# A gated recurrence with a highway layer behind it: a second new order of all operations

## The chip, the cores and the metric

The kernel runs on one core of one Trainium2 chip. The core has TensorE (PE in the profile; PEld is its weight load), VectorE (DVE), ScalarE (ACT), GpSimd (POOL) and SyncE (SP), which here issues nearly all transfers. Each engine works through a queue of its own, in the order in which the program put the instructions there, and waits at semaphores for the others. The metric is the time of one execution on the device in microseconds, the median of several runs; less is better.

## The reference

```python
def _attn_ref(x, f_logit, lower_bound):          # x, f_logit: (4, 6336, 256)
    sig = 1.0 / (1.0 + np.exp(-f_logit))
    f = lower_bound + (1.0 - lower_bound) * sig
    i = 1.0 - f
    h = np.zeros((B, D))
    for t in range(S):
        h = f[:, t] * h + i[:, t] * x[:, t]
        y[:, t] = h

def _moe_ref(x, w_h, w_t, b_t):                  # x = y as (25344, 256)
    H = np.maximum(x @ w_h, 0.0)
    T = 1.0 / (1.0 + np.exp(-(x @ w_t + b_t)))
    return T * H + (1.0 - T) * x
```

Four sequences of 6336 tokens go through a linear recurrence over time, one for each of 256 channels. Its result goes through a highway layer with two 256 x 256 matrices. Reading x and f_logit and writing the output moves 78 MB.

## The kernel before

The 25,344 tokens are cut into 29 **units**: two of 2 blocks of 128 tokens, three of 4 blocks, twenty-two of 8 blocks (units 5 to 26), one of 4 and one of 2. A full unit has 1024 tokens. The 256 channels are two halves of 128, so most operations exist twice per unit. An operation is written as a letter, the unit and the half: `f20.1` is operation f of unit 20 for half 1.

- `l`, `x` (line 257, or 253 for units 0 and 1, which share one transfer): SP loads f_logit and x, tokens on the partitions. `wh` and `wt` load the matrices.
- `u` (line 269): ACT makes sigmoid(-f_logit), which is 1 - sig.
- `b` (line 277): u times x, on POOL, or on DVE where the order has a `v` behind the name.
- `i` (line 285) and `p` (line 305): PE transposes u and b, so that channels lie on the partitions and time runs along the columns. Both write into two PSUM banks, a0 and a1.
- `f` (line 296 on ACT, 294 on DVE with `v`): the forget gate from the transposed u. It needs `ncc` (line 196), which is made from the transposed lower bound (`pc`, `cc`).
- `s` (line 324): DVE runs the scan over time; unit n needs unit n-1. The profile names it TENSOR_TENSOR_SCAN, the lists of the order below SCALAR_TENSOR_TENSOR y.
- `z` and `g` (line 336, and 111 for the second 512 columns): PE multiplies with w_t and w_h. `WHa` and `WTa` (line 224) scale the matrices on ACT first; `IW` (line 208) subtracts the identity from w_h on POOL.
- `t` (line 349): ACT's sigmoid of z. `d` (line 353): DVE's maximum with g.
- `e` (line 359): d times t, on POOL, or on DVE with `v`, in one to three column pieces per unit.
- `o` (lines 381, 382): PE transposes y (times `diag`, which holds cc) and d back and adds them. `c` (line 394 on ACT, 392 on DVE with `v`): the copy out of PSUM. `w` (line 398): SP stores four blocks, half a megabyte (128 KB in unit 28).
- `k*m`: m dummy matmuls on zeros in front of the next PSUM tile (lines 122 and 111).

What sets the order is one string, `order` (lines 49 to 95), a list of 848 such names. The loop at line 401 walks through it and calls `do_<letter>` for each; `pin` keeps every engine's queue in this order. The number behind a colon is the slot: the buffer or PSUM bank that the result goes into, so an operation also waits until the earlier owner of its slot has been read. [...]

Of the kernel before, what the change touches and what calls it, by code (L numbers as in the profile page):

```python
# [53 lines left out]
e1.0v x6:5 b3.0:7 z2.0:1 b4.0:1 f3.0:3 p3.1:1 t2.0:2 d2.0:2 g2.1:0 i4.1:0 o0.0:2 z2.1:1 f4.1:0 s3.1:6 b4.1:0 d2.1 c0.0:0 t2.1 p3.0:1
i4.0:0 f4.0:2 s3.0:7 l7:0 e2.0v p4.0:0 o1.0:2 e2.1 u5:1 p4.1:1 s4.0:0 z3.0:0 l8:1 g3.0:1 t3.0:1 b5.1:3 c1.0:1 i5.1:0 g3.1:0 s4.1:1
i5.0:1 f5.1:1 g4.0:2 d3.0:0 b5.0:2 e3.0 d3.1 p5.1:0 d4.0:1 z4.1:1 z4.0:0 f5.0:3 o2.0:2 p5.0:1 u6:2 c2.0:2 x7:0 s5.1:2 i6.1:0 t4.1:0
g4.1:2 z3.1:1 s5.0:3 f6.1:2 t3.1 t4.0 x8:1 l9:2 d4.1 b6.1:4 p6.1:0 s6.1:4 u7:3 z5.1:1 i6.0:1 f6.0:0 t5.1:2 b6.0:5 g5.0:2 i7.1:0 z5.0:0
p6.0:1 d5.0:2 g5.1:2 u8:0 e4.1 e3.1 e4.0 f7.1v:1 t5.0 l11:3 s6.0:5 d5.1 i7.0:0 o4.0:1 l10:4 x9:2 f7.0:3 b7.0:6 x10:3 p7.0:1 c4.0:3
z6.1:0 b7.1:7 i8.1:0 g6.0:2 b8.1:1 t6.1:1 s7.0:0 b8.0:0 g6.1:1 k*0:a1 d6.0:1 f8.1:2 p7.1:1 e5.2 s7.1:1 d6.1 z6.0:0 i8.0:0 o3.0:2 u9:1
e5.1v t6.0 g7.1:0 i9.0:1 e6.2v e5.0v f8.0:0 e6.1v z7.0:1 c3.0:4 z7.1:2 i9.1:0 w0.0 f9.0:3 w1.0 e6.0v b9.1:3 p8.1:1 t7.0:0 o5.0:1 t7.1  # L60
o5.1:2 f9.1:1 u10:2 c5.0:0 p8.0:0 x11:4 b9.0:2 w4.0 w2.0 d7.1:0 e7.1 g7.0:0 s8.1:6 i10.0:1 o6.0:1 s8.0:7 l13:5 p9.1:0 c5.1:1 z8.0:2
d7.0 f10.0v:2 l12:0 w5.1 u11:3 t8.0:2 e7.2 z8.1:0 w3.0 x12:5 s9.1:2 c6.0:3 b10.0:4 i11.0:1 f11.0:0 w5.0 l14:1 t8.1 g8.1:2 e7.0 p9.0:0
d8.1:2 o6.1:1 l15:2 u13:0 k*1:a1 s9.0:3 g8.0:2 i10.1:1 b11.0:5 d8.0 c6.1:2 f10.1:1 o7.1:0 w6.0 p10.0:0 e8.1 g9.1:1 b10.1:6 c7.1:1
z9.1:2 u12:1 t9.1:1 s10.0:4 i13.1:1 d9.1:1 f13.1:3 g9.0:0 x13:0 p10.1:0 s10.1:5 o7.0:1 e8.0 e8.2 c7.0:4 o8.1:2 p11.0:1 d9.0 i11.1:0
l16:4 z10.1:1 b12.1:7 g10.1:0 c8.1:0 s11.0:0 f11.1:2 z9.0:2 d10.1:0 b11.1:1 p11.1:0 i12.0:1 o8.0:0 u14:2 b12.0:0 t9.0 f12.0:1 w8.1 w6.1
w7.0 s11.1:1 t10.1:0 g10.0:2 k*0:a1 i12.1:1 e9.0 z10.0:1 p12.0:0 b13.0:3 d10.0 f12.1v:0 c8.0:3 u15:3 z11.1:0 z11.0:2 p12.1:1 t10.0
o9.1:1 t11.0:2 b13.1:2 s12.0:6 s12.1:7 t11.1 x14:1 i13.0:0 g11.0:2 d11.0:2 f13.0:2 w8.0 o9.0:0 p13.0:0 c9.1:0 i14.0:1 c9.0:2 s13.0:2
z12.1:1 g11.1:2 e10.0 f14.0:1 d11.1 t12.1:1 b14.0:4 x15:2 u16:1 i14.1:1 b15.1:6 g12.1:0 o10.1:1 z12.0:2 f14.1:0 d12.1:1 p13.1:0 b14.1:5
c10.1:4 g12.0:0 e11.0v i16.0:1 w7.1 l18:3 t12.0 x16:3 s13.1:3 f16.0:2 o10.0:1 c10.0:3 o11.1:2 c11.1:1 p14.0:0 i15.0:1 b15.0:1 w9.1
l17:5 l20:0 d12.0 z13.0:1 g13.1:0 f15.0:3 t13.0:0 p14.1:1 s14.0:4 o11.0:2 i15.1:0 d13.1:0 z13.1:1 s14.1:5 g13.0:0 u18:0 d13.0 f15.1:1  # L70
i18.0:0 b16.0:0 w10.1 p15.1:1 w11.1 x17:4 c11.0:0 t13.1 f18.0:0 z14.0:2 e12.0 t14.0:2 z14.1:0 s15.1:0 p15.0:0 w10.0 t14.1 s15.0:1
o12.0:1 p16.0:1 g14.0:2 c12.0:4 g14.1:0 d14.0:2 i16.1:0 u17:2 w11.0 d14.1 b16.1:7 e13.0 o12.1:1 b17.0:3 s16.0:6 b17.1:2 e14.0 z15.1:2
f16.1:1 c12.1:1 i17.0:0 t15.1:1 f17.0:3 g15.1:0 o13.0:1 d15.1:1 x18:5 p16.1:1 z15.0:2 i17.1:0 g15.0:0 c13.0:3 s16.1:7 l19:1 u20:3
o13.1:1 x19:0 f17.1:2 c13.1:0 p17.0:1 t15.0 b18.0:4 i18.1:0 f18.1:1 g16.0:1 d15.0 g16.1:0 s17.0:2 w12.1 w12.0 d16.0:0 p17.1:1 z16.1:2
z16.0:1 d16.1 u19:1 t16.1:0 x20:1 i19.0:0 t16.0 o14.0:0 f19.0:3 b18.1:5 o14.1:2 l21:2 c14.0:1 s17.1:3 c14.1:4 w9.0 i19.1:1 p18.1:0
z17.1:1 e15.0v z17.0:0 e16.0v g17.1:2 w13.1 b19.0:6 x21:2 f19.1:2 p18.0:1 t17.0:2 t17.1 b19.1:1 s18.1:4 o16.1:0 i20.0:0 u21:2 l22:4
b20.0:0 d17.1:2 s18.0:5 f20.0:1 g17.0:1 o16.0:2 w14.1 w13.0 c16.0:2 i21.1:1 p19.0:0 z18.0:2 d17.0 f21.1:0 c16.1:0 b20.1:7 t18.0:1
p19.1:1 z18.1:1 l23:3 b21.0:3 g18.1:0 t18.1 s19.0:6 s19.1:7 p20.0:0 o15.0:2 b21.1:2 e17.0 o15.1:1 u22:0 d18.1:0 i21.0:1 s20.0:0 g18.0:0
c15.0:4 c15.1:3 z19.0:2 w16.1 d18.0 g19.0:1 x22:3 i20.1:0 f21.0:3 d19.0:1 w15.1 t19.0:0 p20.1:1 w16.0 f20.1:2 z19.1:0 o17.1:2 e18.0
t19.1 g19.1:1 p21.0:0 o17.0:0 s20.1:1 d19.1 w14.0 i22.1:1 b22.1:5 s21.0:2 u23:1 c17.1:0 g20.1:1 o18.0:2 f22.1:1 e19.0 i22.0:1 l24:5  # L80
c17.0:3 x23:4 d20.1:2 w17.1 p21.1:0 o18.1:0 w15.0 c18.0:2 f22.0:2 s21.1:3 g20.0:2 i23.0:1 c18.1:1 u24:2 z20.0:1 t20.0:2 f23.0:3 p22.1:0
d20.0 z20.1:0 b22.0:4 l25:0 w17.0 x24:5 o19.1:2 c19.1:0 s22.1:4 g21.0:1 i23.1:1 p22.0:0 z21.0:2 b23.1:6 w18.1 t20.1 d21.0:0 f23.1:0
b23.0:1 g21.1:1 e20.0 o19.0:0 s22.0:5 t21.0:1 b24.0:0 l26:1 l28:2 c19.0:4 d21.1 i24.0:1 f24.0:1 p23.1:0 z22.1:2 g22.0:1 t22.1:0 z21.1:0
s23.1:6 d22.0:1 i24.1:1 b24.1:7 u25:3 p23.0:0 o20.1:2 s23.0:7 t21.1 x25:0 g22.1:1 c20.1:3 o20.0:0 d22.1 p24.0:0 z22.0:2 e21.0 f24.1:2
c20.0:1 w19.1 b25.0:3 e22.1 g23.1:1 z23.1:0 w20.0 s24.0:0 t22.0 b25.1:2 d23.1:2 p24.1:1 l27:4 s24.1:1 u26:0 t23.1:2 w20.1 i25.0:0
g23.0:2 f25.0:0 o21.1:1 o21.0:0 e22.2 c21.1:0 c21.0:1 i25.1:0 x26:1 p25.0:1 d23.0 f25.1:3 u28:1 g24.1:1 z24.0:2 t24.0:1 s25.0:2 i26.0:0
b26.0:5 d24.1:0 z24.1:0 p25.1:1 f26.0:1 t24.1 e22.0v z23.0:2 x28:2 t23.0 i28.0:0 f28.0:2 o22.0:1 g24.0:0 o22.1:2 c22.0:3 s25.1:3 d24.0
i28.1:0 e23.1 e23.0v w19.0 x27:3 u27:2 i26.1:1 e24.0v w21.1 w21.0 f28.1:0 c22.1:4 g25.0:1 e23.2v b26.1:4 e24.2 o23.0:0 w22.0 f26.1:3
p26.0:0 z25.0:2 d25.0:1 c23.0:0 t25.0:0 o23.1:1 w23.0 w22.1 p26.1:1 s26.0:4 z25.1:0 c23.1:1 w18.0 i27.0:0 o24.1:2 g25.1:1 t25.1 e24.1
s26.1:5 f27.0:1 c24.1:3 i27.1:0 f27.1:3 b27.1:6 d25.1 g26.1:0 z26.1:2 z26.0:1 b27.0:1 p27.0:1 w23.1 e25.1 d26.1:2 o24.0:0 e25.0v  # L90
t26.1:2 t26.0 p27.1:0 c24.0:0 b28.0:0 o25.1:2 e25.2 c25.1:4 s27.0:6 e26.2 w24.1 g26.0:1 s27.1:7 o25.0:0 d26.0 c25.0 z27.0:a1 t27.0:1
p28.0:0 o25.3:2 b28.1:7 s28.0:0 e26.0v g27.1:0 z27.1:1 c25.3:2 e26.1 t27.1 p28.1:1 d27.1:0 s28.1:1 w24.0 o25.2:a0 c25.2 o26.3:2 o26.2:1
c26.3:1 g27.0:0 e27.1v d27.0 e27.0v w25.0 o26.1:a0 w25.1 z28.0:a1 o26.0:2 c26.2 c26.1:3 g28.0:1 t28.0:0 g28.1:0 z28.1:a0 o27.1:a1 c26.0
# [345 lines left out]
```

## Time and profile before

| | |
|---|---|
| median of 3 runs | 206.5 us (206.05 to 206.52) |
| profiled execution: its own time | 206.63 us |
| profiled execution: span | 204.8 us |
| PE busy | 190.2 us (93%) |
| DVE busy | 192.0 us (94%) |
| ACT busy | 194.5 us (95%) |
| POOL busy | 171.8 us (84%) |
| moved by DMA | 78.68 MB, mean 384 GB/s |

The span is what the trace covers; the profiled execution's own time is 1.8 us more. In the chain of work that ended last, PE has 39%, DVE 20%, ACT 15%, POOL 13%, and 10% is issue time. "Busy" counts an instruction from its start to its end; neighbours on one engine overlap by a tenth of a microsecond or so, and the start-to-start time is what the queue really spends on one.

### The profile page before, as it was taken

What the parts mean: (1) busy time and instruction counts of PE and PEld (TensorE: products, weight loads), DVE (VectorE), ACT (ScalarE), POOL (GpSimd) and SP (SyncE); (2) the same over time, 40 slices, a digit from 0 to 9 for tenths busy, and PEclk for the clock granted to TensorE, in tenths of its full rate; (3) what the DMA queues carried; (4) which work ended last, traced back from release to release, by engine and by line L of the source; (5) the groups of instructions that cost most, each with busy time, mean ns of one, the idle gap of its engine ahead of it and who ended that gap; (6) DMA issues with size and microseconds to landing.
All of it is one profiled execution on the core that took longest, in us unless ns stands there. A gap on an engine that the chain in (4) does not pass through costs nothing.

```text
span 204.8 us, 4621 instructions
## 1 busy us (share of the span) xinstructions
PE 190.2 (93%) x1818; PEld 131.8 (64%) x1818; DVE 192.0 (94%) x160; ACT 194.5 (95%) x204; POOL 171.8 (84%) x97
## 2 busy tenths in 40 slices
...
GB/s 196 397 422 416 413 426 413 421 413 414 426 426 413 426 415 422 420 426 417 426 413 426 428 410 419 403 346 337 334 403 412 424 324 381 390 187 402 212 307 261
DMA packets 16381, 78.68 MB, mean 384 GB/s; under 512 B 1764, under 2 KB 2536, under 8 KB 10728
## 3 DMA queue, kind: packets, MB, share of 16 engines
...
q10 hardware_dynamic: 8, 0.00, 0.0%
HBM read 52.43 MB, written 25.95 MB: 383 GB/s over the span
## 4 chain that ended last, share of the span: by engine, by line
PE 39%; DVE 20%; ACT 15%; POOL 13%; issue 10%; ACTq 0%; POOLq 0%; DVEq 0%
DVE y L324 11%; POOL bv L277 8%; DVE d L353 6%; PE op L381 6%; PE op L382 6%; ACT o L394 5%; POOL d L359 5%; PE g L336 5%; PE bT L305 5%; ACT f L296 5%; PE z L336 4%; PE g L111 4%; ACT t L349 4%; PE z L111 4%; PE uT L285 4%
## 5 line engine op out<-in xcount | busy, mean ns | idle before, releaser
L277 POOL TENSOR_TENSOR bv<-u,x 128x1024 bf16<-128x1024 f16 (+2 forms) x53 | 104.8, 2007 | 16.3 <-DVE d L359 5.5
L324 DVE TENSOR_TENSOR_SCAN y<-f,y,bT 128x1024 bf16<-128x1024 f16 (+5 forms) x56 | 107.3, 1930 | 0.7 <-PE bT L305 0.2
L359 POOL TENSOR_TENSOR d<-d,t 128x512 bf16<-128x512 bf16 (+2 forms) x31 | 67.2, 2180 | 3.2 <-DVE d L359 2.4
L353 DVE SCALAR_TENSOR_TENSOR d<-y,ncc,g 128x1024 bf16<-128x1024 bf16 (+2 forms) x58 | 63.5, 1108 | 1.0 <-PE g L111 0.4
L349 ACT ACTIVATE t<-z,bt 128x1024 bf16<-128x1024 f32 (+2 forms) x58 | 60.4, 1088 | 1.0 <-PE z L111 0.8
L296 ACT ACTIVATE f<-uT,ncc 128x1024 f16<-128x1024 f16 (+2 forms) x54 | 59.1, 1097 | 1.2 <-PE uT L285 0.9
L394 ACT COPY o<-op 128x1024 f32<-128x1024 f32 (+2 forms) x57 | 54.0, 994 | 0.8 <-PE op L382 0.6
L269 ACT ACTIVATE u<-l 128x2048 f16<-128x2048 f32 (+2 forms) x29 | 50.5, 1745 | 1.7 <-DMA l<-in_f_logit_dram 1.7
L381 PE MATMUL op<-diag,y 128*128 128x128 f16 x396 | 49.3, 219 | 1.1 <-DVE d L353 0.5
L382 PE MATMUL op<-ident_b,d 128*128 128x128 bf16 x396 | 49.4, 219 | 0.0
L382 PEld LDWEIGHTS <-d 128*128 128x128 bf16 x396 | 44.1, 113 | 3.8 <-issue 1.7
L381 PEld LDWEIGHTS <-y 128*128 128x128 bf16 x396 | 44.2, 113 | 2.2
L336 PE MATMUL g<-y,w_sb 128*128 128x512 bf16 (+1 forms) x116 | 40.2, 368 | 0.8 <-ACT o L394 0.3
L336 PE MATMUL z<-y,w_sb 128*128 128x512 bf16 (+1 forms) x116 | 39.9, 368 | 0.3 <-ACT o L394 0.2
L305 PE MATMUL bT<-ident_f,bv 128*128 128x128 f32 x198 | 32.0, 277 | 4.3 <-ACT f L296 1.4
L285 PEld LDWEIGHTS <-u 128*128 128x128 f16 x396 | 26.3, 98 | 13.2 <-issue 4.9
L285 PE MATMUL uT<-ident_h,u 128*128 128x128 f16 x396 | 31.5, 219 | 2.4 <-DVE y L324 0.9
L111 PE MATMUL g<-y,w_sb 128*128 128x512 bf16 x88 | 33.3, 379 | 0.0
L111 PE MATMUL z<-y,w_sb 128*128 128x512 bf16 x88 | 33.3, 379 | 0.0
L336 PEld LDWEIGHTS <-w_sb 128*128 128x128 f16 x232 | 22.3, 98 | 15.2 <-ACT f L296 0.2
L305 PEld LDWEIGHTS bT<-ident_f,bv 128*128 128x128 f32 x198 | 22.1, 141 | 13.1 <-issue 4.4
L111 PEld LDWEIGHTS <-w_sb 128*128 128x128 f16 x176 | 17.2, 98 | 15.9 <-issue 1.8
...
## 6 DMA issues: line engine op xcount, KB each, us to landing
...
l<-in_f_logit_dram SPq DMA_DIRECT2D x22, 1024.0 KB, 14.1
x<-in_x_dram SPq DMA_DIRECT2D x22, 1024.0 KB, 12.1
...
```

Of the source, the lines that this page charges most:

```text
L111: return pe.add_instruction(mybir.InstMatmult(name=nc.get_next_instruction_name(), start_tensor_calc=start, stop_tensor_calc=stop, tile_si ...
L277: shared(pin(e.tensor_mul(bv[:, :nb // 2].rearrange("p k d j -> p k j d"), st[n]["u"][:, :nb, own].rearrange("p (k j) d -> p k j d", j=2), ...
L285: pin(nc.tensor.transpose(uT[:, j * P:(j + 1) * P], st[n]["u"][:, j, h * P:(h + 1) * P], ident_h))
L296: pin(nc.scalar.activation(to, of, AF.Identity, scale=ncc[:, h:h + 1], bias=1.0))
L305: pin(nc.tensor.transpose(words[:, k:k + g * (P - 1) + 1:g], pair, ident_f))
L324: pin(nc.vector.tensor_tensor_scan(y[:, c:e], st[n]["f", h][:, c:e], st[n]["bT", h][:, c:e], 0.0 if fresh else carry[h], op0=ALU.mult, op1 ...
L336: pin(nc.tensor.matmul(p[:, a:e], w, half(n, "y", ki)[:, a:e], start=ki == 0, stop=ki == NH - 1))
L349: pin(nc.scalar.activation(half(n, "t", m), st[n]["z", m][:, :tokens(n)], AF.Sigmoid, bias=bt[:, m:m + 1]))
L353: pin(nc.vector.scalar_tensor_tensor(half(n, "d", m), half(n, "y", m), ncc[:, m:m + 1], st[n]["g", m][:, :tokens(n)], op0=ALU.mult, op1=AL ...
L359: shared(pin(e.tensor_mul(st[n]["d"][:, a:c], st[n]["d"][:, a:c], st[n]["t"][:, a:c])), not eng)
L381: pin(nc.tensor.matmul(o, half(n, "y", h)[:, cols], diag[:, h], start=True, stop=False))
L382: pin(nc.tensor.matmul(o, half(n, "d", h)[:, cols], ident_b, start=False, stop=True))
```

## The change

Only the string `order` is replaced: the same 29 units and the same functions, with every name in a new place. Slots change with it, and so does the engine of some operations (the `v` moves).

```diff
@@ -47,51 +47,51 @@
     order = """
-k*3:a0 l0:0 pc:0 x0:0 cc u0:0 k*3:1 pb:2 i0.0:1 k*4:0 dg wh u1:1 b0.1v:0 f0.0:0 b0.0v:1 i1.0:0 l2:1 wt IW f1.0v:1 p0.0:1 WHa cb i0.1:0
...
-d28.0:1 t28.1 d28.1 w26.1 w26.0 e28.0v c27.1:0 o27.0:1 e28.1v o28.0:2 c28.0:4 o28.1:a0 w28.0 c28.1:2 w28.1 c27.0 w27.0
+k*3:a0 l0:0 k*4:0 u0:0 pb:1 x0:0 pc:2 i0.0:1 cc k*1:0 u1:1 b0.1:0 dg wh l2:1 f0.0:0 i1.1:0 b0.0v:1 i0.1:1 b1.1v:2 b1.0:3 f1.1:1 l3:2
...
+s28.1:3 o26.2:2 g27.0:a0 o26.1:1 e27.1v c26.2 o26.0:a1 z28.1:0 d27.0 g28.0:2 w25.0 c26.1:0 e27.0v c26.0 d28.0:1 o27.0:1 o27.1:a0
+c27.0v:2 t28.1:2 g28.1:a1 z28.0:2 d28.1 c27.1 t28.0 e28.1v w26.1 e28.0v w26.0 o28.1:0 c28.1:1 o28.0:1 c28.0:4 w27.0 w28.1 w28.0
 """
```

Counted over the whole string, these operations change their engine. From DVE to POOL: b0.1, b1.0, b2.1 and e0.0, e0.1, e1.0, e1.1, e2.0, e5.0, e5.1, e22.0, e23.0, e23.2, e25.0. From POOL to DVE: e7.0, e7.2, e9.0, e19.0. From DVE to ACT: f1.0, f10.0. From ACT to DVE: f2.0, f3.0, f4.0, c25.2, c27.0. The dummy matmuls of `k` go from 19 to 13.

The loads at the start, on SP, before:

```order
L253 DMA l<-in_f_logit_dram 128x2x512
L253 DMA x<-in_x_dram 128x2x512
L186 DMA w_raw<-in_moe_w_h_dram 128x2x256
L257 DMA l<-in_f_logit_dram 128x1024
L183 DMA w_raw<-in_moe_w_t_dram 128x2x256
L257 DMA x<-in_x_dram 128x1024
L257 DMA l<-in_f_logit_dram 128x1024
L257 DMA x<-in_x_dram 128x1024
```

and now:

```order
L253 DMA l<-in_f_logit_dram 128x2x512
L253 DMA x<-in_x_dram 128x2x512
L186 DMA w_raw<-in_moe_w_h_dram 128x2x256
L257 DMA l<-in_f_logit_dram 128x1024 x2
L257 DMA x<-in_x_dram 128x1024
L183 DMA w_raw<-in_moe_w_t_dram 128x2x256
L257 DMA x<-in_x_dram 128x1024
```

f_logit of unit 3 has moved ahead of w_t and of x of unit 2, and w_t behind both.

DVE's queue at the start, from the first b on, before:

```order
L277 TENSOR_TENSOR bv<-u,x 128x2x128 x2
L294 TENSOR_SCALAR f<-uT,ncc 128x256
L203 COPY bt<-tbT 128x2
L324 SCALAR_TENSOR_TENSOR y<-f,bT 128x256
L277 TENSOR_TENSOR bv<-u,x 128x2x128 x2
L324 SCALAR_TENSOR_TENSOR y<-f,bT 128x256
L324 SCALAR_TENSOR_TENSOR y<-f,y,bT 128x256 x2
L353 SCALAR_TENSOR_TENSOR d<-y,ncc,g 128x256 x2
L277 TENSOR_TENSOR bv<-u,x 128x2x2x128
L353 SCALAR_TENSOR_TENSOR d<-y,ncc,g 128x256 x2
L324 SCALAR_TENSOR_TENSOR y<-f,y,bT 128x512 x2
L359 TENSOR_TENSOR d<-d,t 128x256 x4
```

and now:

```order
L277 TENSOR_TENSOR bv<-u,x 128x2x128 x2
L203 COPY bt<-tbT 128x2
L324 SCALAR_TENSOR_TENSOR y<-f,bT 128x256 x2
L324 SCALAR_TENSOR_TENSOR y<-f,y,bT 128x256 x2
L294 TENSOR_SCALAR f<-uT,ncc 128x512
L353 SCALAR_TENSOR_TENSOR d<-y,ncc,g 128x256
L294 TENSOR_SCALAR f<-uT,ncc 128x512
L353 SCALAR_TENSOR_TENSOR d<-y,ncc,g 128x256
L324 SCALAR_TENSOR_TENSOR y<-f,y,bT 128x512
L353 SCALAR_TENSOR_TENSOR d<-y,ncc,g 128x256
L324 SCALAR_TENSOR_TENSOR y<-f,y,bT 128x512
L353 SCALAR_TENSOR_TENSOR d<-y,ncc,g 128x256
```

The four scans of units 0 and 1 stand together; f1.0, three b and four e have left this queue, and f2.0 and f3.0 (512 columns) have come.

DVE's queue near the end, from e24.0 on, now (the copy in line 392 is c25.2):

```order
L359 TENSOR_TENSOR d<-d,t 128x1024
L353 SCALAR_TENSOR_TENSOR d<-y,ncc,g 128x1024
L324 SCALAR_TENSOR_TENSOR y<-f,y,bT 128x1024 x2
L353 SCALAR_TENSOR_TENSOR d<-y,ncc,g 128x1024 x2
L324 SCALAR_TENSOR_TENSOR y<-f,y,bT 128x512
L392 COPY o<-op 128x512
L324 SCALAR_TENSOR_TENSOR y<-f,y,bT 128x512
L353 SCALAR_TENSOR_TENSOR d<-y,ncc,g 128x1024
```

and POOL's queue now, from the e22.0 that it has taken over:

```order
L359 TENSOR_TENSOR d<-d,t 128x1024
L359 TENSOR_TENSOR d<-d,t 128x512 x3
L277 TENSOR_TENSOR bv<-u,x 128x4x2x128
L359 TENSOR_TENSOR d<-d,t 128x512
L359 TENSOR_TENSOR d<-d,t 128x1024
L277 TENSOR_TENSOR bv<-u,x 128x4x2x128
L277 TENSOR_TENSOR bv<-u,x 128x2x2x128
L359 TENSOR_TENSOR d<-d,t 128x512
L277 TENSOR_TENSOR bv<-u,x 128x2x2x128
L359 TENSOR_TENSOR d<-d,t 128x1024
L359 TENSOR_TENSOR d<-d,t 128x512 x3
```

Before, the copy was on ACT, and DVE went in this place from s26.1 over d25.1, d26.1 and e25.0 straight to the two scans of unit 27.

More of the change, by code (lines that the diff above doesn't have):

```diff
@@ L54 @@
[L54 to L93, printed above, removed]
@@ new lines @@
+d0.0:1 p2.0:1 s2.1:4 d0.1 z1.0:0 z1.1:2 b3.0:6 b3.1:7 g1.0:1 i4.0:0 s2.0:5 t1.1:1 e1.1 d1.0 z0.1:2 x4:3 t0.1 p3.0:1 z2.1:1 f4.0v:2 l5:4
+b4.1:1 e0.0 i4.1:0 g2.1:2 t1.0 s3.0:6 t2.1:2 p3.1:1 e1.0 f4.1:0 x5:4 e0.1 p4.1:0 o1.0:0 d2.1:2 s3.1:7 s4.1:2 g2.0:1 u5:1 b4.0:0 d2.0
+c1.0:0 z2.0:2 l6:5 i5.1:1 o0.0:0 t2.0 p4.0:0 z3.1:2 x6:5 g3.0:1 b5.1:3 f5.1:3 b5.0:2 t3.1:1 i5.0:1 s4.0:3 g4.1:2 l7:0 e2.0 p5.1:0
+d3.0:0 d4.1:1 z3.0:1 s5.1:0 e2.1 c0.0:1 z4.0:0 f5.0:1 z4.1:2 u6:2 p5.0:1 l8:1 b6.1:4 t4.1:0 s5.0:1 t4.0 t3.0 i6.1:0 g4.0:2 o2.0:0 d4.0
```

41 lines of the change are left out of this document (38 added, 3 removed).

## The prediction

> **What bounds the kernel now.** The first view is busy time by stretch of the span, because an average over the run hides where an engine is full.
>
> ```profile
> core 0: us, PE busy (x) PEld busy (x) DVE busy (x) ACT busy (x) POOL busy (x), PEclk, DMA share, GB/s
> 5.00:10.00 5.00, 4.30 (x22) 1.91 (x20) 3.11 (x8) 3.37 (x8) 0.87 (x2) 1.00 1.06 397
> 20.00:60.00 40.00, 35.77 (x338) 24.61 (x339) 39.97 (x34) 40.00 (x38) 35.81 (x22) 1.00 1.01 418
> 120.00:140.00 20.00, 19.39 (x192) 13.67 (x190) 19.70 (x13) 20.00 (x20) 17.08 (x9) 1.00 0.95 383
> 180.00:195.00 15.00, 14.91 (x148) 10.60 (x147) 14.61 (x14) 13.73 (x18) 11.36 (x10) 1.00 0.66 261
> 200.00:204.80 4.80, 0.14 (x3) 0.00 (x0) 0.00 (x0) 1.14 (x3) 0.00 (x0) 1.00 0.67 255
> ```
>
> Between 20 and 60 us DVE is busy for 39.97 and ACT for 40.00 of 40 us; between 120 and 140 us for 19.70 and 20.00 of 20. There are thus two full engines side by side. Idle time lies at the ends: in 5 to 10 us DVE lacks 1.89 and ACT 1.63, and after 200 us only ACT's 1.14 us of copies and the last stores are left. The DMA engines are full too for long, so I looked next at who waits for them, and at the biggest waits of POOL.
>
> ```profile
> POOL bv L277 <- DVE d L359: 5.5, 3, 3.2
> ACT u L269 <- DMA l<-in_f_logit_dram: 1.7, 1, 1.7
> POOL bv L277 <- DMA x<-in_x_dram: 1.0, 1, 1.0
> ```
>
> The list of waits puts only 1.7 us (the first load, at the start) and 1.0 us (one load near the end) on loads, so the transfers run ahead of their users. [...] The third view is the chain of waits around 140 us, where the two full engines meet.
>
> ```profile
> 139.90 1.01 ACT f L296
> 140.92 0.03 issue
> 140.94 1.73 DVE y L324
> ```
>
> This is f20.1 on ACT, released into scan s20.1 on DVE with 0.03 us between. So at 140 us ACT, not DVE, sets the pace. A gain must therefore arrive on ACT up to there, and on DVE behind it.
>
> **The change, part one: work that goes to another engine.** Durations are those of the groups by form.
>
> ```profile
> L296 ACT ACTIVATE f<-uT,ncc 128x1024 f16<-128x1024 f16 x41 | 50.8, 1242 | 0.0
> L296 ACT ACTIVATE f<-uT,ncc 128x512 f16<-128x512 f16 x8 | 5.7, 727 | 0.3
> L296 ACT ACTIVATE f<-uT,ncc 128x256 f16<-128x256 f16 x5 | 2.5, 505 | 0.9 <-PE uT L285 0.9
> L394 ACT COPY o<-op 128x512 f32<-128x512 f32 x12 | 6.9, 592 | 0.6 <-PE op L382 0.4 <-ACT o L394 0.2
> L294 DVE TENSOR_SCALAR f<-uT,ncc 128x1024 f16<-128x1024 f16 x3 | 3.8, 1280 | 0.0
> L294 DVE TENSOR_SCALAR f<-uT,ncc 128x256 f16<-128x256 f16 x1 | 0.5, 485 | 0.8 <-PE uT L285 0.8
> L277 DVE TENSOR_TENSOR bv<-u,x 128x256 bf16<-128x256 f16 x4 | 1.5, 439 | 1.2 <-DMA x<-in_x_dram 1.2
> L277 DVE TENSOR_TENSOR bv<-u,x 128x512 bf16<-128x512 f16 x1 | 0.7, 721 | 0.0
> L359 DVE TENSOR_TENSOR d<-d,t 128x2048 bf16<-128x2048 bf16 x3 | 3.6, 1214 | 0.0
> L359 DVE TENSOR_TENSOR d<-d,t 128x1024 bf16<-128x1024 bf16 x7 | 4.7, 682 | 0.0
> L359 DVE TENSOR_TENSOR d<-d,t 128x512 bf16<-128x512 bf16 x7 | 2.8, 414 | 0.0
> L359 DVE TENSOR_TENSOR d<-d,t 128x256 bf16<-128x256 bf16 x6 | 1.4, 283 | 0.0
> L353 DVE SCALAR_TENSOR_TENSOR d<-y,ncc,g 128x512 bf16<-128x512 bf16 x8 | 5.7, 738 | 0.1
> L359 POOL TENSOR_TENSOR d<-d,t 128x1024 bf16<-128x1024 bf16 x2 | 4.3, 2137 | 0.0
> L359 POOL TENSOR_TENSOR d<-d,t 128x512 bf16<-128x512 bf16 x19 | 21.9, 1167 | 3.1 <-DVE d L359 2.4 <-DVE d L353 0.6
> ```
>
> ACT loses three f of 512 columns (2.0, 3.0, 4.0) and two copies of 512 (c25.2, c27.0), and takes f1.0 (256) and f10.0 (1024): -3 x 0.73 - 2 x 0.59 + 0.51 + 1.24 = -1.6 us of durations. Instructions overlap by some 0.14 us each in the records, so ACT gets about 1.3 us free.
>
> DVE loses f1.0 and f10.0 (1.77), three b (2 x 0.44 + 0.72 = 1.60) and eleven e (4 x 0.28 + 3 x 0.41 + 4 x 0.68 = 5.1). It takes four e (0.41 + 0.68 + 2 x 1.21 = 3.5), three f of 512 and two copies of 512. No row shows the last two forms on DVE. An f lies between 0.49 (256 columns) and 1.28 (1024); I take 0.75. A copy lies between 0.41 (512 columns, bf16) and 1.28; I take 0.70, near the d of 512 columns (0.738), which reads the same kind of PSUM tile. The sum is -8.5 + 3.5 + 2.25 + 1.4 = -1.35, and since two neighbours overlap by 0.08 us (two scans of 2.34 take 4.58 below), seven instructions fewer leave about -0.8. The bounds of the two unknown forms move it from -2.1 to +2.0. POOL takes the three b and eleven e and gives four e: about +5.4 us, with e at 1.17 for 512 and 2.14 for 1024 columns. Its cover is its own waiting: it is not full before 60 us nor after 120.
>
> **Part two: the head.** These rows date it.
>
> ```profile
> 2.44 0.63 PE L122 MATMUL idle<-zeros 128*128 128x512 bf16 x1
> 2.87 1.06 PE L111 MATMUL idle<-zeros 128*128 128x512 bf16 x2
> 8.31 0.38 PE L122 MATMUL idle<-zeros 128*128 128x512 bf16 x1
> 8.13 0.68 DVE L324 TENSOR_TENSOR_SCAN y<-f,bT 128x256 bf16<-128x256 f16 x1
> 25.51 4.58 DVE L324 TENSOR_TENSOR_SCAN y<-f,y,bT 128x1024 bf16<-128x1024 f16 x2
> 9.54 1.05 ACT L269 ACTIVATE u<-l 128x1024 f16<-128x1024 f32 x1
> 25.36 1.91 ACT L269 ACTIVATE u<-l 128x2048 f16<-128x2048 f32 x1
> ```
>
> An early dummy matmul takes 0.43 us from start to start (2.44 to 2.87). Both kernels issue 13 before about 7.5 us, but now seven stand ahead of the transposes of the constants, so cc comes at about 6.0 and f0.0 at about 6.3. Then f1.1, f0.1, f1.0 follow on ACT, each behind a transpose, and s0.0 starts at about 8.3 (before: 8.13). In exchange the four scans of units 0 and 1 follow without the two b between them, and from s0.0 to s5.1 (the first scan of 1024, at 25.51) DVE's list is 1.2 us shorter. One of these is no gain: one more d of 512 now waits behind s5.1. With 0.15 us of waits I get s5.1 at 24.4, 1.1 earlier. ACT's list from u2 to u6 (9.54 and 25.36 before) is 0.9 shorter, and u2 starts 1.1 earlier since the scaling of w_h no longer stands ahead. Against that I count 0.6 us more waiting, f2.1 and f3.1 for PSUM banks that DVE frees late. So u6 starts at 23.9, 1.45 earlier.
>
> The reordered loads I cost at nothing. At 397 GB/s a half-megabyte load passes in 1.3 us, so x of unit 2 lands about 0.7 us later, w_t 2.6 us later at about 11.3, f_logit of unit 3 2 us earlier. The new place of the scaling of w_t is behind f2.1, at 11.8 by the same walk. If that cover were gone, z0 and the t behind it would move by up to 0.8 us.
>
> [...]
>
> **Part three: the middle.** ACT needed 115.55 us from u6 to the end of f20.1 (25.36 to 140.91). Its list is now the same plus f10.0, about 1.0 us, so f20.1 ends at 23.9 + 115.55 + 1.0 = 140.5. DVE's list from s5.1 to s20.1 is 0.6 longer (e9.0 and two e of unit 7 come, f10.0 and two e of unit 5 go), and it sat idle some 0.7 us in this stretch; unhindered it would be there at about 139.7. So ACT still decides, and s20.1 starts at 140.5 instead of 140.94. What was 1.45 us at 24 us has shrunk to 0.4.
>
> From s20.1 to the end of e26.0 DVE needed 54.35 us. Its list there is 0.3 shorter (four e out, e19.0, c25.2 in).
>
> **Part four: a new meeting at c25.2.** This copy stands in DVE's queue behind s27.1, ahead of s27.0. It needs o25.2 on PE, and that needs e25.2 on POOL. POOL must first wait for e24.0 on DVE (the port order), then do b26.1, b27.0, e24.2, b27.1, e25.0, e25.2. By the durations this is about 8.7 us plus 0.6 for PE. DVE meanwhile has three d and two scans of 1024 columns and one scan of 512, about 9.25. The two are equal, so I book 0.3 us of waiting, which uses up the 0.3 gained. e26.0 then ends at 140.5 + 54.35 = 194.9, less about 0.3 for small waits before the scans of unit 27 that have more room now: 194.6.
>
> **Part five: the tail.**
>
> ```profile
> 194.63 0.67 DVE L359 TENSOR_TENSOR d<-d,t 128x1024 bf16<-128x1024 bf16 x1
> 200.00 1.14 ACT L394 COPY o<-op 128x256 f32<-128x256 f32 x3 [0.20 <-PE op L382]
> DMA to landing us min/median/max: 1.8/2.7/3.2
> ```
>
> Now e26.0 ends at 195.3, and 9.5 us follow. The last instructions on ACT are c28.0, c28.1 and c27.0, and the last store is half a megabyte for unit 27 (2.7 us to landing). In the new order c27.0 is on DVE earlier, that store goes ahead, and the last one is 128 KB of unit 28 (1.8). Against this, s28.0 and c27.0 now stand behind e26.0 on DVE. Step by step from the end of e26.0: c27.0 starts at 3.45 (it waits 0.3 for PE), e28.0 ends at 5.2, c28.0 at 6.3, its store is issued at 6.4, lands at 8.2, and 0.75 us close the program: 8.95, a gain of 0.55.
>
> The sum: 194.6 + 8.95 = 203.55 against a span of 204.8, thus -1.25 us (0.4 in the middle, 0.3 behind it, 0.55 in the tail). The profiled execution took 206.63, 0.13 over the median of 206.50, so the forecast for the median is **205.3 us**. A change within 0.3% (205.9 to 207.1) could not be told from none.
>
> **Rivals.** *The middle eats it.* The head gains nothing that reaches 140 us if ACT waits 0.4 us or more between 24 and 140; it lost nothing there before, though f20.1 arrived with 0.03 us to spare. With 0.9 us of such waits the result is 206.2. For it speaks that both engines are full, so that any wait is paid for; against it, that POOL feeds earlier.
>
> *POOL comes late to c25.2: slower.* Place: DVE's queue at about 189 us. POOL has 5.4 us more work, and its margin at e25.2 is about nil. Every us that POOL loses between e24.0 and e25.2 stops DVE, with s27.0 and all of units 26 to 28 behind it. Beyond 1.9 us of such waiting the kernel is more than 0.3% slower; POOL had waited 1.6 us for DVE and 1.0 us for a load in this region. With 2.4 us, about those two together, it gives 207.7. Against it: a busier POOL waits less for its inputs.
>
> [...]
>
> *The new waits do not occur.* If the small stalls before the scans of units 25 to 27 (0.6 us) and at c25.2 go, 204.4.
>
> **How the numbers follow.** Forecast 0.46 (204.6 to 205.9); no new waits 0.14 (about 204.4); the middle eats it 0.15; the slow TensorE 0.05; POOL late 0.20. Faster are the first two, less 0.02 that falls over the bound: 0.58. Same: 0.22. Slower: 0.20. The range leaves out about a tenth at each end: from 203.9 (0.5 below the case without waits, since the f and the copy on DVE may be as short as their lower bounds) to 207.5 (half of the case of a late POOL). For the forecast alone it is 204.6 to 205.9.
>
> **What would show it.** Right: u6 on ACT near 23.9, s5.1 near 24.4, s20.1 near 140.5 directly behind f20.1, c25.2 on DVE with a wait under 0.5 us, a last store of 128 KB, and a span near 203.5. Wrong: s0.0 after 8.6; ACT with idle time between 24 and 140; a gap before c25.2 of over 1 us on DVE; f of 512 on DVE near 1 us.

## The result

The changed kernel takes 207.72 us, the median of 14 executions, against 206.16 for the kernel before, also of 14 on the same chip: a ratio of 1.0063 with a 95% interval of 1.0047 to 1.008. By the medians it is slower by 1.6 us, where 1.25 us less were forecast. (The kernel before was at 206.50 in the prediction, the median of 3.)

The 14 times are not spread evenly. Three lie at 206.0 to 206.8, eleven at 207.4 to 208.0, and nothing lies between. The profiled execution is one of the three: 206.40 us with a span of 204.6. Its dates can therefore be set against the prediction, but it does not show the loss. For that I had the same kernel profiled again (the first experiment).

### The profile page after: what moved, and what is told of

Read it like the earlier page. It is cut to its first block, busy times and chain, and to the rows that moved or that the text cites. A ratio compares the mean times of both kernels' runs of the same rounds, so it can differ in the third digit from the quotient of the medians.

```text
span 204.6 us, 4609 instructions
## 1 busy us (share of the span) xinstructions
PE 188.0 (92%) x1812; PEld 131.1 (64%) x1812; DVE 192.3 (94%) x153; ACT 193.2 (94%) x201; POOL 177.2 (87%) x107
## 4 chain that ended last, share of the span: by engine, by line
PE 57%; DVE 27%; issue 8%; ACT 5%; ACTq 0%; DVEq 0%
DVE y L324 18%; PE bT L305 8%; PE z L336 7%; PE op L382 7%; PE g L336 7%; PE op L381 7%; DVE d L353 7%; PE uT L285 6%; PE z L111 6%; PE g L111 6%; ACT f L296 2%; ACT o L394 2%; PE idle L111 1%; DVE f L294 1%; ACT u L269 1%
## 5 line engine op out<-in xcount | busy, mean ns | idle before, releaser
L277 POOL TENSOR_TENSOR bv<-u,x 128x1024 bf16<-128x1024 f16 (+2 forms) x56 | 106.9, 1932 | 15.4 <-DVE d L359 6.1
L359 POOL TENSOR_TENSOR d<-d,t 128x512 bf16<-128x512 bf16 (+3 forms) x38 | 69.7, 1850 | 2.5 <-ACT t L349 1.6
L349 ACT ACTIVATE t<-z,bt 128x1024 bf16<-128x1024 f32 (+2 forms) x58 | 59.5, 1055 | 1.1 <-POOL bv L277 0.5
L296 ACT ACTIVATE f<-uT,ncc 128x1024 f16<-128x1024 f16 (+2 forms) x53 | 56.5, 1077 | 1.6 <-PE uT L285 0.8
L394 ACT COPY o<-op 128x1024 f32<-128x1024 f32 (+2 forms) x55 | 52.1, 980 | 2.4 <-PE op L382 1.5
L269 ACT ACTIVATE u<-l 128x2048 f16<-128x2048 f32 (+2 forms) x29 | 49.8, 1719 | 1.6 <-DMA l<-in_f_logit_dram 1.6
L305 PE MATMUL bT<-ident_f,bv 128*128 128x128 f32 x198 | 31.4, 276 | 5.4 <-DVE y L324 3.8
```

What stands on the lines that cost most here:

```text
L277: shared(pin(e.tensor_mul(bv[:, :nb // 2].rearrange("p k d j -> p k j d"), st[n]["u"][:, :nb, own].rearrange("p (k j) d -> p k j d", j=2), ...
L296: pin(nc.scalar.activation(to, of, AF.Identity, scale=ncc[:, h:h + 1], bias=1.0))
L305: pin(nc.tensor.transpose(words[:, k:k + g * (P - 1) + 1:g], pair, ident_f))
L349: pin(nc.scalar.activation(half(n, "t", m), st[n]["z", m][:, :tokens(n)], AF.Sigmoid, bias=bt[:, m:m + 1]))
L359: shared(pin(e.tensor_mul(st[n]["d"][:, a:c], st[n]["d"][:, a:c], st[n]["t"][:, a:c])), not eng)
```

## The profile after

First the dates that the prediction named, from the timeline of the changed kernel (start, duration, engine, line, operation, what it writes and reads, how many; in brackets the idle time in front and what ended it). The first two rows are s0.0 with s1.0 behind it, and s5.1; then u6; then f20.1 on ACT and s20.1 on DVE; then s27.1, c25.2 and s27.0.

```profile
7.79 1.29 DVE L324 TENSOR_TENSOR_SCAN y<-f,bT 128x256 bf16<-128x256 f16 x2 [0.19 <-PE bT L305]
24.50 4.58 DVE L324 TENSOR_TENSOR_SCAN y<-f,y,bT 128x1024 bf16<-128x1024 f16 x2
24.35 1.92 ACT L269 ACTIVATE u<-l 128x2048 f16<-128x2048 f32 x1
139.39 1.35 ACT L296 ACTIVATE f<-uT,ncc 128x1024 f16<-128x1024 f16 x1
140.77 2.35 DVE L324 TENSOR_TENSOR_SCAN y<-f,y,bT 128x1024 bf16<-128x1024 f16 x1
189.01 1.27 DVE L324 TENSOR_TENSOR_SCAN y<-f,y,bT 128x512 bf16<-128x512 f16 x1
190.20 0.66 DVE L392 COPY o<-op 128x512 f32<-128x512 f32 x1
190.83 1.28 DVE L324 TENSOR_TENSOR_SCAN y<-f,y,bT 128x512 bf16<-128x512 f16 x1
```

s5.1 came at 24.50 (24.4 forecast), u6 at 24.35 (23.9), f20.1 ended at 140.74 with s20.1 0.03 us behind it (140.5). The copy c25.2 started right behind s27.1, with no wait in front. From the group of its form: an f of 512 columns on DVE took 0.740 us (0.75 was chosen), a copy of 512 columns 0.678 (0.70).

The end of the run, on DVE and then ACT, from d27.0, with the row on the last transfers (from issue to landing):

```profile
196.32 0.75 DVE L353 SCALAR_TENSOR_TENSOR d<-y,ncc,g 128x512 bf16<-128x512 bf16 x1
197.18 0.42 DVE L359 TENSOR_TENSOR d<-d,t 128x512 bf16<-128x512 bf16 x1
197.72 0.48 DVE L353 SCALAR_TENSOR_TENSOR d<-y,ncc,g 128x256 bf16<-128x256 bf16 x1
198.28 0.69 DVE L392 COPY o<-op 128x512 f32<-128x512 f32 x1
198.95 0.48 DVE L353 SCALAR_TENSOR_TENSOR d<-y,ncc,g 128x256 bf16<-128x256 bf16 x1
199.53 0.52 DVE L359 TENSOR_TENSOR d<-d,t 128x256 bf16<-128x256 bf16 x2
200.54 0.65 ACT L394 COPY o<-op 128x256 f32<-128x256 f32 x2 [0.81 <-ACT t L349]
DMA to landing us min/median/max: 2.4/2.5/3.7
```

e26.0 (`193.86 0.74`) ended at 194.60, as forecast. From there e28.0 ended 5.45 us later (5.2 forecast), c28.0 6.6 (6.3), and the span 10.0 (8.95 with the closing 0.75). So even this faster group has only 0.2 us of gain in the span, because the tail took 1.05 us more than its term. The last store of 128 KB took 2.4 us to land where I had 1.8; the half megabyte of unit 27, issued just before the last two stores, took 3.7.

## The experiments

**The changed kernel again, unaltered.** Two further profiles, to see an execution of the larger group.

> The changed kernel once more, nothing left out. Its 14 executions lie in two groups: three at 206.0 to 206.8 us and eleven at 207.4 to 208.0, and the trace at hand is of the lower group (206.4). Theory A (the stall theory): the upper group has one more wait of about 1.3 us at one place in the middle or the tail; a trace of that group shows the engines as in the trace at hand up to some point and 1.3 us later from there on. Theory B (the clock theory): TensorE's full clock is granted at another time after the start; then the whole head is later, s0.0 at 8.3 us or after (7.79 in the trace at hand) and every later point by the same amount. Expected 207.7 us.

> The changed kernel again, nothing left out, for another trace. As for the run before it: theory A expects a trace of 207.6 us with a lag that begins at one place behind the head, theory B a trace that is late from the first scan on.

Measured: 207.69 us (10 executions; ratio 1.0052, 1.0026 to 1.0078), profiled at 207.28; and 207.89 for one further execution. The ten times fall into the same two groups, three at 205.9 to 206.6 and seven at 207.3 to 208.0. Both profiles have the head of the faster execution to within 0.2 us (s5.1 at 24.51 and 24.67, u6 at 24.36 and 24.52). At s20.1 they are 1.35 and 1.15 us behind it. Where it happens is seen between 85 and 95 us. First the faster execution, DVE and then POOL:

```profile
86.08 4.59 DVE L324 TENSOR_TENSOR_SCAN y<-f,y,bT 128x1024 bf16<-128x1024 f16 x2
90.59 1.20 DVE L359 TENSOR_TENSOR d<-d,t 128x2048 bf16<-128x2048 bf16 x1
91.70 2.34 DVE L324 TENSOR_TENSOR_SCAN y<-f,y,bT 128x1024 bf16<-128x1024 f16 x1
90.55 5.35 POOL L277 TENSOR_TENSOR bv<-u,x 128x1024 bf16<-128x1024 f16 x2 [0.37 <-DMA x<-in_x_dram]
```

and the same place in the second profile of the same kernel, with two rows from the list of waits of this stretch:

```profile
86.15 4.58 DVE L324 TENSOR_TENSOR_SCAN y<-f,y,bT 128x1024 bf16<-128x1024 f16 x2
90.65 3.09 DVE L359 TENSOR_TENSOR d<-d,t 128x2048 bf16<-128x2048 bf16 x1
93.66 2.33 DVE L324 TENSOR_TENSOR_SCAN y<-f,y,bT 128x1024 bf16<-128x1024 f16 x1
90.52 2.14 POOL L277 TENSOR_TENSOR bv<-u,x 128x1024 bf16<-128x1024 f16 x1 [0.30 <-PE op L382]
93.91 2.14 POOL L277 TENSOR_TENSOR bv<-u,x 128x1024 bf16<-128x1024 f16 x1 [1.25 <-DVE d L359]
PE uT L285 <- DVE y L324: 1.5, 1, 1.5
POOL bv L277 <- DVE d L359: 1.2, 1, 1.2
```

The row of 1.20 and of 3.09 us is the same instruction, e11.0 on DVE. In the second profile b16.1 on POOL started at 90.52, 0.13 us ahead of it, and ended at 92.66. e11.0 was not done until 1.08 us after that, about its own length: it waited for the whole of b16.1, inside its recorded duration. Scan s14.0 came 1.96 us later than in the faster execution. A transposition on PE waits 1.5 us for DVE, and ACT's next t then waits 0.83 us for its product z. The further execution shows the same: b16.1 ended at 92.46, and e11.0, which started at 90.78, took 2.76 us, again to 1.08 us after that end. In the faster execution the two start within 0.04 us of each other, e11.0 keeps its 1.20 us, and it is POOL that pays: two b take 5.35 us where two take 4.25 in the third experiment's profile below.

The same shows in the group of e with 2048 columns on DVE, faster execution first, then the second profile:

```profile
L359 DVE TENSOR_TENSOR d<-d,t 128x2048 bf16<-128x2048 bf16 x5 | 5.9, 1204 | 0.0
```

```profile
L359 DVE TENSOR_TENSOR d<-d,t 128x2048 bf16<-128x2048 bf16 x5 | 8.0, 1615 | 0.0
```

So in these profiles e11.0 and b16.1 exclude each other, in either direction: one keeps its time (b16.1 2.14 us in the second profile, e11.0 1.20 in the faster execution), and the other pays within its recorded duration (e11.0 1.9 us, POOL 1.1). What the two engines share no profile shows; the kernel has `shared port` as the reason of the waits that `shared` (line 174) sets. All other waits of this kernel follow from data and slots. `shared` guards one direction alone: it makes a POOL operation wait for the DVE operation (b, e or `dg`) that stands last before it in the order. b16.1 stands ahead of e11.0 in the order, so nothing keeps it from going first, and x of unit 16 lands at just the time when s13.1 ends (in the faster execution b16.1, released by that load, started at 90.55, and s13.1 ended at 90.67).

**The loads of the start as before**, in the changed order.

```diff
-wh l2:1 f0.0:0 ... f1.1:1 l3:2 k*2:2 ... s1.0:2 x2:1 k*0:a0 ... b2.1:4 wt u3:3
+wh l2:1 wt x2:1 l3:2 f0.0:0 ... f1.1:1 k*2:2 ... s1.0:2 k*0:a0 ... b2.1:4 u3:3
```

> The changed order, with only the first loads put back as they were before: w_t and x of unit 2 ahead of f_logit of unit 3. If the place of f_logit matters, f_logit of unit 3 lands at about 11.35 us and not at 9.4, u3 (9.61 us in the changed kernel's trace) waits for it, and since it stands ahead of f2.1 and the scaling of w_t on ACT, ACT loses about 1.3 to 1.7 us; u6 then starts at about 25.7 instead of 24.35, s20.1 behind f20.1 about 1.3 us later, and the kernel takes 1.0 to 1.5 us more than the changed one. If the head's lead is lost in the middle anyway (the rival that the middle eats it), the time differs by less than 0.4 us.

Measured: 209.24 us (209.03 to 210.15; ratio 1.0152, 1.0128 to 1.0176), 1.55 over the changed kernel beside it. The list of waits of the first 30 us on ACT and the timeline on DVE:

```profile
ACT u L269 <- DMA l<-in_f_logit_dram: 1.6, 2, 1.4
```

```profile
13.24 0.75 DVE L294 TENSOR_SCALAR f<-uT,ncc 128x512 f16<-128x512 f16 x1 [1.26 <-PE uT L285]
```

u3 waits 1.44 us for f_logit of unit 3, f3.0 on DVE 1.26 behind it, u6 starts at 26.47 (25.7 expected), and s5.1 comes at 26.63. So the new order of operations needs the new order of loads.

**The new loads alone**, in the order of before.

```diff
-l2:1 wt IW ... f0.1:2 x2:1 b1.1v:2 ... p1.1:0 l3:2 g0.0:1
+l2:1 l3:2 x2:1 wt IW ... f0.1:2 b1.1v:2 ... p1.1:0 g0.0:1
```

> The kernel before with one part of the change alone: f_logit of unit 3 loaded ahead of x of unit 2 and w_t. In its trace u3 starts at 13.06 us, 1.7 us after its data landed, and b2.1 at 12.14, 2 us after x of unit 2 landed; only the scaling of w_t (10.49, data at 8.8) would now wait, for data at about 11.3, which delays ACT by about 0.8 us. By the view that the order of loads has its worth only together with the new order on ACT: no gain, 206.2 to 207.0. The rival, that early f_logit is worth something by itself, expects 205.7 or less.

Measured: 206.99 us (ratio 1.004, 1.0025 to 1.0056).

```profile
ACT w_sb L224 <- DMA w_raw<-in_moe_w_t_dram: 1.5, 1, 1.5
```

The scaling of w_t on ACT waits 1.5 us, at its old place (it starts at 11.38); in the changed order the scaling has moved behind f2.1 and this wait is gone. Alone, either half of the head loses; together they bring s5.1 from 25.51 to 24.50. Of that, 0.34 us are an earlier s0.0 (7.79, before 8.13), a date that differs from one execution to the next (last section).

**The two copies back on ACT.**

```diff
-c25.2v ... c27.0v:2
+c25.2 ... c27.0:2
```

> The changed order, with only the copies c25.2 and c27.0 back on ACT, in the same places. If the meeting at c25.2 on DVE and the longer list behind it cost the tail, DVE's list after s20.1 is 1.35 us shorter and its waits of 0.4 us before d26.1 to c25.2 and 0.2 before c27.0 go: 0.5 to 1.0 us less than the changed kernel. The rival, that the end is set by ACT's copies and the store of unit 27, expects no gain or a loss of up to 0.5 us, since two copies of 0.47 us join ACT's queue. If the upper group of times comes from c25.2 on DVE, it is gone here and the median falls by about 1.3 us more.

Measured: 207.75 us (207.62 to 208.19; ratio 1.0075, 1.006 to 1.009), no gain. DVE loses two copies and waits instead. On DVE, 195 to 203 us:

```profile
DVE d L359 <- ACT t L349: 0.7, 2, 0.6
DVE d L353 <- PE g L336: 0.7, 1, 0.7
```

e28.0 ends 6.2 us after e26.0 instead of 5.45. The copies on DVE are not what costs the time, and c25.2 had no wait to give back. Nor do they make the larger group: all four times lie in it, and e11.0 takes 2.91 us in this profile.

**b16.1 behind e11.0.** One name moved in the string: b16.1 then stands behind e11.0, and `shared` makes it wait.

```diff
-b15.0:6 b16.1:1 t12.0 ... e11.0v i16.0:0
+b15.0:6 t12.0 ... e11.0v b16.1:1 i16.0:0
```

> The changed order with one move: POOL's b16.1 stands behind e11.0 (on DVE) in the list, so that it waits for it; before, it stood ahead and started at 90.52 us, just before e11.0 at 90.65. Port theory: e11.0 on DVE and b16.1 on POOL exclude each other, whoever comes second waits for the other's end; in most executions b16.1 is first by a tenth of a microsecond and e11.0 takes 3.09 us instead of 1.20. With the move e11.0 takes 1.2 us in every execution, POOL starts b16.1 at about 91.8, and all executions lie at 205.9 to 206.8 us: median about 206.2, 1.4 less than the changed kernel and equal to the kernel before. Rival, the load theory: the upper group comes from the late landing of x of unit 16 (90.3 to 90.5 us); then the move only delays POOL, and the median stays at 207.6 or rises.

**x of unit 16 loaded earlier**, ahead of two stores, which should help if the late load was the fault, and should not if the meeting was.

```diff
-x15:2 u14:1 ... b14.0:5 x16:3 z12.1:2
+x15:2 x16:3 u14:1 ... b14.0:5 z12.1:2
```

> The changed order with only the load of x of unit 16 issued earlier, directly behind that of unit 15 and ahead of two stores. Its data land some 1.3 to 2.5 us earlier, so POOL starts b16.1 right behind b15.0, at about 90.2 us, and no longer at 90.5. Port theory: POOL is now always first, e11.0 on DVE (free at 90.6) waits for the end of b16.1 at about 92.3 and takes some 2.8 us; all executions lie in the upper group, 207.4 to 208.0, although the data come earlier. Load theory: the upper group goes, median 206.2.

These two ran side by side. With b16.1 behind e11.0: 206.30 us (12 executions, 205.53 to 207.56; ratio 1.0002, 0.9987 to 1.0018). One execution of twelve is over 207, where it was eleven of fourteen, and the kernel is level with the one before. (The spread is wider than the 205.9 to 206.8 expected, and what made the one slow execution is open: no profile of it was taken.) With x of unit 16 earlier: 207.33 (206.90 to 207.45; ratio 1.0052, 1.0038 to 1.0067), with no execution under 206.9. DVE and POOL of the first, then of the second:

```profile
90.34 1.20 DVE L359 TENSOR_TENSOR d<-d,t 128x2048 bf16<-128x2048 bf16 x1
91.46 2.34 DVE L324 TENSOR_TENSOR_SCAN y<-f,y,bT 128x1024 bf16<-128x1024 f16 x1
91.77 4.25 POOL L277 TENSOR_TENSOR bv<-u,x 128x1024 bf16<-128x1024 f16 x2 [1.93 <-ACT f L296]
```

```profile
85.94 6.36 POOL L277 TENSOR_TENSOR bv<-u,x 128x1024 bf16<-128x1024 f16 x3
90.68 2.70 DVE L359 TENSOR_TENSOR d<-d,t 128x2048 bf16<-128x2048 bf16 x1
93.31 2.33 DVE L324 TENSOR_TENSOR_SCAN y<-f,y,bT 128x1024 bf16<-128x1024 f16 x1
```

Earlier data lets POOL run three b in one piece, so b16.1 (the third, from 90.16) is already running when e11.0 comes at 90.68, and e11.0 takes 2.70 us. The 1.9 us that POOL stands still in the other kernel cost nothing. In all five profiles where b16.1 went first by over 0.1 us (two of the unaltered kernel, this one, the loads as before and the copies on ACT), e11.0 ended 1.07 to 1.08 us after it. This is the cause of the loss against the kernel before: about 1.4 us, 207.7 to 206.3 (the kernel before beside them: 206.22 and 206.32).

**ACT's head on top of it**: b16.1 as above, and two names of the head moved so that ACT gets through it with less waiting.

```diff
-d1.0 z0.1:2 ... g2.1:2 t1.0 s3.0:6 ... t2.0 p4.0:0 z3.1:2 x6:5
+d1.0 t1.0 z0.1:2 ... g2.1:2 s3.0:6 ... t2.0 z3.1:2 p4.0:0 x6:5
```

> As the run with b16.1 behind e11.0, and in addition two waits of ACT near 16 and 22 us taken away: t1.0 stands ahead of t0.1 (which waited 0.5 us for z0.1), and z3.1 ahead of p4.0 on PE (t3.1 waited 0.5 us for it behind a transpose that waits for POOL). ACT gets about 1.0 us; if ACT sets the pace up to f20.1, as in the prediction, s20.1 comes up to 0.9 us earlier and the kernel takes 205.3 to 205.6. If DVE has no slack there either, the gain over the run with b16.1 alone is under 0.4 us.

Measured: 206.42 us (205.63 to 208.3; ratio 1.0009, 0.9989 to 1.0028). u6 starts at 23.84, the 23.9 of the prediction; f20.1 and s20.1 do not come sooner. Its timeline, with s5.1 in the second row:

```profile
23.84 1.91 ACT L269 ACTIVATE u<-l 128x2048 f16<-128x2048 f32 x1
24.33 4.58 DVE L324 TENSOR_TENSOR_SCAN y<-f,y,bT 128x1024 bf16<-128x1024 f16 x2
139.26 1.36 ACT L296 ACTIVATE f<-uT,ncc 128x1024 f16<-128x1024 f16 x1
140.66 2.35 DVE L324 TENSOR_TENSOR_SCAN y<-f,y,bT 128x1024 bf16<-128x1024 f16 x1
```

Without the two names u6 came at 24.07, s5.1 at 24.17 and s20.1 at 140.56. ACT's 0.23 us have not arrived. DVE needs from s5.1 to s20.1 116.33 us here, 116.39 without the two names and 116.27 in the first profile of the changed kernel: the same, however early ACT is (in the two kernels of the tail below it is 116.77 and 116.41). This speaks for DVE as the engine that sets the pace of the middle in the new order. With a lead of 0.23 us and one profile of each it is not shown.

**The tail.** Two orders, both with b16.1 behind e11.0. In the first, PE does g28.1 and z28.0 ahead of the output products of unit 27, ACT does t28.0 ahead of c27.1, and DVE does c27.0 last; in the second only PE's order is changed.

```diff
-d28.0:1 o27.0:1 o27.1:a0 c27.0v:2 t28.1:2 g28.1:a1 z28.0:2 d28.1 c27.1 t28.0 e28.1v w26.1 e28.0v w26.0
+d28.0:1 g28.1:a1 z28.0:2 o27.0:1 o27.1:a0 t28.1:2 d28.1 t28.0 c27.1:2 e28.1v w26.1 e28.0v c27.0v w26.0
```

> As with b16.1 behind e11.0, and in the tail TensorE does the products g28.1 and z28.0 ahead of the output products o27.0 and o27.1, ACT does t28.0 ahead of the copy c27.1, and DVE does the copy c27.0 (0.69 us) behind e28.0 and no longer between d28.0 and d28.1. Theory (the tail was longer than forecast because the copy on DVE and the two output products stand ahead of unit 28's last chain): d28.1 starts right behind d28.0, e28.0 ends about 0.6 us sooner (4.8 to 4.9 behind the end of e26.0 where it was 5.45), c28.0 ends near 5.9 behind it instead of 6.58, and the time is 0.4 to 0.6 us less than with b16.1 alone moved: about 205.8, ratio to before 0.997 to 0.998. Rival (the last stores set the end, not the last chain): the store of unit 27 is now issued near 200.3 instead of 199.2 and takes its 2.4 to 3.7 us, so that it lands last, and the time stays within 0.2 of 206.3 or goes over it.

```diff
-d28.0:1 o27.0:1 o27.1:a0 c27.0v:2 t28.1:2 g28.1:a1 z28.0:2 d28.1
+d28.0:1 g28.1:a1 z28.0:2 o27.0:1 o27.1:a0 c27.0v:2 t28.1:2 d28.1
```

> As with b16.1 behind e11.0, and of the tail only the order on TensorE is changed: g28.1 and z28.0 ahead of o27.0 and o27.1; the copy c27.0 stays between d28.0 and d28.1 on DVE. Theory (the copy alone holds the chain): d28.1 still starts right behind the copy, e28.0 ends 5.3 to 5.45 us behind the end of e26.0, and the time stays at 206.2 to 206.4, ratio to before 1.000. Rival (TensorE's order is what holds it): e28.0 ends near 4.9 behind e26.0 and the time is 0.4 us less.

Measured: 206.62 us (12 executions; ratio 1.0008, 0.9996 to 1.002) and 206.72 (10; 1.0018, 1.0003 to 1.0034). The first, DVE, ACT, and its last transfers with their size and time to landing:

```profile
198.56 1.07 DVE L353 SCALAR_TENSOR_TENSOR d<-y,ncc,g 128x256 bf16<-128x256 bf16 x2
199.73 0.58 DVE L359 TENSOR_TENSOR d<-d,t 128x256 bf16<-128x256 bf16 x2
200.45 1.35 ACT L394 COPY o<-op 128x512 f32<-128x512 f32 x3 [0.46 <-PE op L382]
out_dram<-o SPq DMA_DIRECT2D x2, 128.0 KB, 2.5
```

and the transfers of the kernel with b16.1 moved alone:

```profile
out_dram<-o SPq DMA_DIRECT2D x2, 128.0 KB, 1.8
```

The chain of unit 28 did get shorter: e28.0 ended at 200.31, 4.87 us after the end of e26.0. But the copy c27.1 now runs behind the chain, c28.0 comes 6.36 after e26.0 (6.58 before), the half megabyte of unit 27 goes out 5.6 us after e26.0 instead of 4.8, and the last 128 KB take 2.5 us instead of 1.8. The gain is given back. The rival had the time and the late store right; but it is still a store of unit 28 that lands last. In the second, neither expectation was right: with PE's order changed the copy c27.0 itself waits for its products,

```profile
198.80 0.69 DVE L392 COPY o<-op 128x512 f32<-128x512 f32 x1 [0.92 <-PE op L382]
```

and stands ahead of d28.1, so that e28.0 ends 6.3 us after e26.0. No version beat the kernel before.

## Why the prediction was wrong

**The failed step.** Parts one and three priced every e and b by the mean of its group and added them up engine by engine. The step left out that an e on DVE and a b on POOL that meet exclude each other (shown for e11.0 with b16.1, and in the order before with b15.1), so the pair has a price that depends on which is first: e11.0 stood for the 1.21 us of its group, and in the larger group of times it takes 2.76 to 3.09. The prediction treated the order that `shared` imposes (its "port order") as one that makes POOL wait, where cover was at hand; that DVE waits for POOL in the opposite case it did not consider, though the list of waits of before had 5.5 us of b on POOL waiting for an e on DVE. In the order before, b15.1 stood ahead of e11.0 in the same unguarded way. There e11.0 came at 88.14 as b14.0 ended, and b15.1 paid 1.0 us on POOL (five b in 11.65 us, where five times 2.13 are 10.65), which moved nothing on DVE:

```profile
88.14 1.22 DVE L359 TENSOR_TENSOR d<-d,t 128x2048 bf16<-128x2048 bf16 x1
89.28 2.34 DVE L324 TENSOR_TENSOR_SCAN y<-f,y,bT 128x1024 bf16<-128x1024 f16 x1
86.09 11.65 POOL L277 TENSOR_TENSOR bv<-u,x 128x1024 bf16<-128x1024 f16 x5
```

Those rows are of the kernel before. The new order brings e11.0 and b16.1 together within 0.04 to 0.5 us. By the two groups of times POOL wins in most executions (the profiles show one of the faster group and two of the larger), and 1.4 us are lost; moving one name takes this away.

**The tail** (part five) had the right path and a wrong size: 10.0 us from e26.0 in the first profile, 9.3 to 9.4 where the last store lands in 1.8 us, against 8.95. About 0.3 are in the copies and c28.0, the rest is the landing. With the tail in one and the same order, the half megabyte of unit 27 took 3.0 to 3.1 us and the last store 1.8 in four profiles, 3.7 to 3.8 and 2.4 to 2.5 in two (the first one and the further execution). In all six the last store was issued while that half megabyte was still under way and landed 0.6 to 0.7 us behind it. What holds up the half megabyte in some executions stays open. The forecast gain of 0.55 shrinks to 0.1 to 0.2, or turns into a loss of 0.5.

**The head, the middle and the meeting at c25.2** (parts two to four) have dates that came out as forecast within 0.5 us: s5.1 +0.1, u6 +0.45, s20.1 +0.27, e26.0 +0.0, in the execution without the collision. For the head this is luck in part. s0.0 started at 7.79 where 8.3 was forecast, and from s0.0 to s5.1 DVE took 16.71 us where the forecast had 16.1, so two errors of half a microsecond cancel. In all nine profiles with the new order of loads and operations this stretch takes 16.6 to 16.9 us, with s0.0 anywhere from 7.26 to 8.20: the term of the head is mis-sized by 0.6 us. Some 0.3 of it is idle time of DVE, which was 0.47 us between 8.2 and 24.1 us in the first profile where 0.15 of waits were booked; where the rest lies stays open. (The prediction also reads only 1.7 and 1.0 us of waits on loads; the same list has 4.6 us of POOL for w_h and 1.2 of DVE for x, both at the start.)

In part three ACT's term was near: 116.39 us from u6 to the end of f20.1, where 115.55 + 1.0 were booked. DVE's was not. Its list grew by 0.57 us, as counted, but the 0.7 us of idle time that the walk dropped stayed for the most part (from 24.5 to 140.7 us DVE was idle 0.65 before and 0.54 now), and s5.1 to s20.1 took 116.3 us where the walk gave 115.3. So the two engines come to s20.1 together, and an earlier u6 alone brought nothing. The prices of f and copy on DVE were right to 0.02 us.

**The rivals.** "POOL late to c25.2" had 207.7 at a chance of 0.20. The number is what was measured, but by luck, since the mechanism is not: c25.2 waited for nothing. It was right that DVE would stop for POOL, and wrong about the place (90 us, not 189) and the mechanism (the exclusion, not a late input). "The middle eats it" is nearest to the kernel without the collision (206.2 against 206.3), though in the profiles the head and the tail fall short too, by more than the 0.2 to 0.3 us of the middle. For the slow TensorE, at a chance of 0.05, no run shows that the new order prolongs the slow start: the first dummy matmul of 0.38 us starts at 5.82 in the first profile, at 8.31 before. How long the slow start lasts differs from one execution to the next (to about 4 us in one profile and about 7 in another, in the last section).

**The sum.** In us, stage by stage; the collision lies in the third row.

| | before | forecast | first profile | second profile | b16.1 moved |
|---|---|---|---|---|---|
| to s0.0 | 8.13 | 8.3 | 7.79 | 7.72 | 7.31 |
| s0.0 to s5.1 | 17.38 | 16.1 | 16.71 | 16.79 | 16.86 |
| s5.1 to s20.1 | 115.43 | 116.1 | 116.27 | 117.61 | 116.39 |
| s20.1 to the end of e26.0 | 54.36 | 54.1 | 53.83 | 54.00 | 53.83 |
| to the end of the span | 9.5 | 8.95 | 10.0 | 9.4 | 9.35 |
| span | 204.8 | 203.55 | 204.6 | 205.5 | 203.7 |

Measured 207.7 against 205.3, thus 2.4 us; against the kernel before beside it, +1.6 instead of -1.25, thus 2.8. The collision is 1.4, the head 0.6, the tail 0.4 to 1.05, and 0.3 came back behind s20.1. That is about the size of the miss, but not a proof, since it sets single profiles against medians. The profiled execution with b16.1 moved has nearly the span that was forecast, and took 205.53 us. It was the fastest of twelve, its s0.0 came 1.0 us sooner than booked, and the median of that kernel is 0.8 higher. To go from one profile to the median with a step of 0.13 us was finer than executions that spread over 0.9 us (the kernel before) and 2.0 (b16.1 moved) allow.
